# Two partial products in the array's two row halves, and a new instruction sequence, in a gated S4D and spectral filter kernel

## The chip, the cores and the metric

The kernel runs on one core of one Trainium2 chip. The metric is the device time of one execution in microseconds. Three runs of the kernel before took 536.1 to 537.85 us, with a median of 536.78 us.

A core has five engines that each work through a list of instructions in order: PE (the matmul array, with its weight loads listed as PEld), DVE (vector), ACT (scalar), POOL (GpSimd) and SP (which only issues transfers here). They wait for each other by semaphores. PE writes to PSUM, which is divided into banks of 512 f32 columns by 128 partitions; DVE and ACT read the results out of it.

## The reference

For x of 2048 positions and 640 channels, a gate g mixes two long filters: an S4D state space convolution along the positions, whose kernel K is generated from 128 complex modes per channel, and a two-dimensional spectral filter.

```python
def _A_ref(u, log_A_real, A_imag, C_real, C_imag, log_dt, D_skip):
    dt = jnp.exp(log_dt)
    A = -jnp.exp(log_A_real) + 1j * A_imag
    C = (C_real + 1j * C_imag) * dt[:, None]
    P = jnp.exp((A * dt[:, None])[:, :, None] * pos[None, None, :])
    K = 2.0 * jnp.einsum("dn,dnl->dl", C, P).real
    y = irfft(rfft(u_t, 2 * L) * rfft(K, 2 * L))[:, :, :L]
    return y + u * D_skip

def _B_ref(x, w_r, w_i):
    X = rfft2(x, axes=(-2, -1)) * (w_r + 1j * w_i)
    return irfft2(X, s=(S, D), axes=(-2, -1))

g = sigmoid((x * gate_w).sum(-1, keepdims=True))
return g * _A_ref(x, ...) + (1 - g) * _B_ref(x, ...)
```

## The kernel before

All Fourier transforms are products with constant tables in f32 on PE. The transform of 4096 points along the positions is factored into 32 x 64 plus a table: `stage1` (L367) and `stage2` (L380) make it, and the inverse is L886 followed by L960 and L172.

The program has these parts. `phase_p` turns the S4D parameters into phases and magnitudes, by DVE and POOL, with an exponential, an arctangent and a logarithm on ACT (L309, L326, L349). `phase_b` generates K in 40 steps: L696 and L706 make arguments on PE in bf16, L697, L712 and L718 take exponentials and sines on ACT, L726 to L732 multiply on DVE and POOL, L745 sums on PE. `phase_a` transforms u (four quarters of the channels, two u tiles each) and sums the gate (L454). Its copies out of PSUM are at L415, on ACT for the first two quarters. `phase_c` and `phase_d` transform K, multiply, go back, and mix.

The second half of `phase_a` is the spectral filter, and this is where the change lies. It runs over nine groups of up to 128 rows (17 blocks of 64). `front` loads a group and folds its 640 channels by symmetry into four planes of 321 numbers, 161 of one symmetry and 160 of the other. `transposes` (L550) brings these onto partitions, in three chunks that `CH` names: 0 to 128, 193 to 321, and the rest 128 to 193. The rest holds the last 33 rows of the first symmetry and the first 32 of the second, 65 rows together. `channels` makes the transform of the channels: for each of the four planes one bank `p_d`, with two results of 161 and 160 columns in it. Each result is a product over a full chunk (L566, 128 rows) plus a product over the 65-row rest (L567), whose table has zeros where the other symmetry lies. ACT copies two of the four banks (L571), DVE adds and subtracts the others (L573, L576). `filt` multiplies by the filter on DVE and folds again (L598, L599, and one column by POOL at L597). The way back is the same: `transposes` with `back=True`, `back1` with L611 (full) and L612 (rest) into `p_eo`, a copy on ACT (L615) and two DVE instructions (L617, L618) that make `qq`; then `back2` (L626, L627) and a transfer. The pool behind `p_t`, `p_d`, `p_eo` and `p_i` has three banks.

```python
v = p[:nl, 161 * par:161 + 160 * par]
P.matmul(v, st.ft[:, c, x, :nl], tab[0], start=True, stop=False)
P.matmul(v, st.ft[:65, 2, x, :nl], tab[1], start=False, stop=True)
```

The shape in which the array is used differs along PE's list: whole for L550, L566, L567, L611, L612 and L626, two row halves of 64 for L696 and L706 (two records, `j` 0 and 1, on partitions 0 and 64, into two banks), two column halves for L367, L380 and L886, four column quarters for L745 and L454.

The order of the instructions on each engine isn't that of the code. `arrange` takes tables, `ORDER` for each engine and `CROSS` between engines, and chains all instructions as they say. So every stream above is interleaved by hand-laid tables, and the tables are different for the two kernels.

Of the kernel before, what the change touches and what calls it, by code (L numbers as in the profile page):

```python
# [9 lines left out]
F32 = mybir.dt.float32  # L10
# [3 lines left out]
ALU = mybir.AluOpType  # L14
# [29 lines left out]
CH = ((0, 128), (193, 321), (128, 193))  # L44
# [5 lines left out]
def _tables():  # L50
# [45 lines left out]
    def chunks(t, part):  # L96
        z = np.zeros((161, t.shape[1]))
# [287 lines left out]
def phase_a(tc, A, T):  # L385
# [97 lines left out]
    with ExitStack() as ctx:  # L483
# [11 lines left out]
        for n in (161, 160) * 4:  # L495
            tabs.append((td[:, o:o + n], td[0:65, o + n:o + 2 * n]))
            o += 2 * n
# [5 lines left out]
        def bank(name):  # L503
            return ps.tile([128, 512], F32, tag="f", name=name)

        def tile5(name, n=E):
            return w4.tile([128, 4, E + 1], F32, tag="f", name=name)[:, :, 0:n]

        def front(pr, st):
# [12 lines left out]
            st.fo = wg.tile([128, 4, E], F32, tag="fg", name="fg")  # L522
            fg = st.fo.rearrange("p (t r) e -> p t r e", t=2)

            def folds(eng, t):
                ins = eng.tensor_tensor(out=fg[:nl, t, :, 1:160], in0=fo[:nl, t, :, 1:160], in1=fo[:nl, t, :, 319:160:-1], op=ALU.add)
                eng.tensor_tensor(out=fg[:nl, t, :, 162:321], in0=fo[:nl, 1 - t, :, 1:160], in1=fo[:nl, 1 - t, :, 319:160:-1], op=ALU.subtract)
# [29 lines left out]

        def channels(st, rest):
            nl = st.nl
            bc = wb.tile([128, 2, E], F32, tag="bc", name="bc")  # L560
            xx = st.xx = tile5("xx").rearrange("p (a b) e -> p a b e", a=2)
            for dst, x, w in ((0, 3, 1), (1, 2, 1), (2, 0, 0), (3, 1, 0)):
                p = bank("p_d")
                for par, (tab, c) in enumerate(fwd[w]):
                    v = p[:nl, 161 * par:161 + 160 * par]
                    P.matmul(v, st.ft[:, c, x, :nl], tab[0], start=True, stop=False)  # L566
                    P.matmul(v, st.ft[:65, 2, x, :nl], tab[1], start=False, stop=True)  # L567
                    yield 0.54
                i = dst % 2
                if dst < 2:  # L570
                    S.copy(bc[:nl, i], p[:nl, :E])  # L571
                else:
                    ins = V.tensor_tensor(out=xx[:nl, 0, i], in0=p[:nl, :E], in1=bc[:nl, i], op=ALU.add)  # L573
                    if dst == 2 and rest:
                        rest(ins)
                    V.tensor_tensor(out=xx[:nl, 1, i], in0=p[:nl, :E], in1=bc[:nl, i], op=ALU.subtract)  # L576

        def filt(st):
# [15 lines left out]
            ff = st.pm = tile5("ff")  # L594
            half = lambda t, i, n: t[:nl, :, i:i + 2 * n].rearrange("p x (b i) -> p x b i", b=2)
            lo, hi = half(pm, 0, 161)[:, :, :, 0:80], half(pm, 1, 160)[:, :, :, :79:-1]
            G.tensor_copy(ff[:nl, :, 160], pm[:nl, :, 80])  # L597
            V.tensor_tensor(out=half(ff, 0, 80), in0=lo, in1=hi, op=ALU.add)  # L598
            V.tensor_tensor(out=half(ff, 161, 80), in0=lo, in1=hi, op=ALU.subtract)  # L599

        def back1(st, j):
# [4 lines left out]
            blocks = lambda t, i, n: t[:, i:i + 2 * n].rearrange("p (b i) -> p b i", b=2)[:, :, 0:160]  # L606
            for w in (1, 0):
                p = bank("p_eo")
                for par, (tab, c) in enumerate(bwd[w]):
                    v = p[:, 161 * par:161 + 160 * par]  # L610
                    P.matmul(v, st.pmt[:, c, w, j, :], tab[0], start=True, stop=False)  # L611
                    P.matmul(v, st.pmt[:65, 2, w, j, :], tab[1], start=False, stop=True)  # L612
                    yield 0.57
                if w:
                    S.copy(o[:, :E], p[:, :E])  # L615
                else:
                    V.scalar_tensor_tensor(out=qv[:, :, 0:160], in0=blocks(o, 0, 161), scalar=T.sg[0], in1=blocks(p, 0, 161), op0=ALU.mult, op1=ALU.add)  # L617
                    V.scalar_tensor_tensor(out=qv[:, :, 319:159:-1], in0=blocks(o, 1, 160), scalar=T.sg[1], in1=blocks(p, 1, 160), op0=ALU.mult, op1=ALU.add)  # L618
# [521 lines left out]
```

## Time and profile before

| what | us |
|---|---|
| median of three runs | 536.78 |
| profiled execution | 540.0 |
| its span, first to last instruction | 538.2 |
| PE busy | 498.8 |
| DVE busy | 421.6 |
| ACT busy | 306.7 |
| POOL busy | 271.0 |

Busy times overlap between engines, so they don't add up to the span. A busy PE is not a PE at its peak: the records of matmuls are pipelined, and each one's duration is longer than the distance to the next. A row of the timeline has the start, the duration of a run of equal instructions, the engine, the line, the operation, what is written and read, the count, and in brackets how long the engine had stood idle before and who ended that. An f32 product is one instruction of the program and two records in the profile.

### The profile page before, as it was taken

The numbers are of one execution on the slowest core, as the hardware profiler recorded it, in microseconds if no ns is written. First come the engines' busy times: TensorE is split into PE (matmuls) and PEld (weight loads), VectorE is DVE, ScalarE is ACT, GpSimd is POOL, SyncE is SP. The second block draws the span as 40 slices with busy tenths as digits, with TensorE's granted clock in tenths as the row PEclk, the third lists the DMA queues.
The fourth block names the chain that finished last, engine by engine and source line by source line (L and its number), as shares of the span: only waits on it lengthen the run. The fifth ranks groups of instructions, "written<-read, shape, count | busy, mean of one in ns | idle before, by whom it ended". The sixth has DMA issues, their size and how long they took to land.

```text
span 538.2 us, 17116 instructions
## 1 busy us (share of the span) xinstructions
PE 498.8 (93%) x7432; PEld 382.1 (71%) x7432; DVE 421.6 (78%) x644; ACT 306.7 (57%) x469; POOL 271.0 (50%) x285
## 2 busy tenths in 40 slices
PE   6499999998889999999999999999999999998865
PEld 4489957765657767767667777667989988975621
DVE  0895448767989998989799789763797979887853
ACT  2386375564985887886977976876333333322100
POOL 4059827246355437375265363173553627674840
PEclk9699999999979999999999999999999999998997
DMA  8665933165550250553322231157779797698964
GB/s 339 233 212 184 333 138 130 46 206 173 187 199 13 63 166 6 167 182 97 83 62 71 99 111 27 55 212 307 263 252 329 258 357 234 191 384 334 311 226 182
DMA packets 47666, 99.89 MB, mean 186 GB/s; under 512 B 3588, under 2 KB 33048, under 8 KB 45928
## 3 DMA queue, kind: packets, MB, share of 16 engines
q1 hardware_dynamic: 25544, 67.08, 36.1%
q10 hardware_dynamic: 19552, 22.19, 12.7%
q0 software_dynamic: 2496, 9.54, 5.1%
q8 instruction: 58, 0.95, 0.8%
q14 instruction: 16, 0.13, 0.1%
HBM read 59.47 MB, written 38.99 MB: 183 GB/s over the span
## 4 chain that ended last, share of the span: by engine, by line
PE 74%; DMA 11%; ACT 7%; DVE 5%; issue 2%; ACTq 1%; POOL 0%; DVEq 0%; SPq 0%; POOLq 0%
PE p_s L367 13%; PE p_s L380 12%; PE p_p L706 8%; PE p_k L745 6%; PE p_i L886 6%; PE p_d L566 4%; PE p_i L626 4%; PE p_t L550 4%; PE p_d L567 3%; PE p_eo L611 3%; DMA s_d<-s 3%; PE p_e L696 3%; PE p_c L960 3%; PE p_eo L612 3%; DMA t<-s_d 2%; DMA lar<-in_la_l 2%
## 5 line engine op out<-in xcount | busy, mean ns | idle before, releaser
L380 PE MATMUL p_s<-t,w 128*64 128x160 f32 x1056 | 88.4, 306 | 0.8 <-ACT ut L415 0.7
L380 PEld LDWEIGHTS p_s<-t,w 128*64 128x64 f32 x1056 | 75.0, 135 | 11.8 <-issue 4.4
L731 POOL TENSOR_TENSOR y<-e,sc 128x512 f32<-128x512 f32 x40 | 52.1, 1303 | 30.1 <-ACT sc L712 24.5
L697 ACT ACTIVATE e<-p_e 128x1024 f32<-128x1024 f32 (+1 forms) x80 | 61.9, 818 | 7.8 <-PE p_e L696 4.9
L732 POOL TENSOR_TENSOR y<-e,sc 128x512 f32<-128x512 f32 x40 | 52.5, 1314 | 26.8 <-ACT sc L712 23.0
L706 PE MATMUL p_p<-rp,par 64*128 64x512 bf16 x480 | 62.6, 384 | 3.6 <-DVE x L728 3.5
L718 ACT ACTIVATE p_p<-p_p 128x1024 f32<-128x1024 f32 x40 | 40.4, 1010 | 34.2 <-PE p_p L706 23.7
L368 ACT COPY t<-p_s 128x512 f32<-128x512 f32 x40 | 25.1, 627 | 50.8 <-PE p_s L367 49.2
L367 PE MATMUL p_s<-c,u 128*64 128x128 f32 x640 | 41.3, 285 | 10.3 <-ACT t L415 9.5
L728 DVE TENSOR_TENSOR x<-e,p_p 128x1024 f32<-128x1024 f32 x40 | 48.5, 1212 | 0.0
L367 PEld LDWEIGHTS p_s<-c,u 128*64 128x64 f32 x640 | 37.7, 143 | 13.9 <-ACT t L415 9.7
L862 POOL TENSOR_TENSOR t<-ma 64x320 f32<-64x320 f32 x32 | 28.6, 893 | 36.0 <-DVE ma L856 34.6
L745 PEld LDWEIGHTS p_k<-x,y 128*32 128x32 f32 x2560 | 37.6, 110 | 10.8 <-issue 10.4
L726 DVE SCALAR_TENSOR_TENSOR x<-e,p_p 128x512 f32<-128x512 f32 x40 | 27.3, 682 | 22.8 <-ACT p_p L718 22.7
L367 PE MATMUL p_s<-c,kt 128*64 128x128 f32 x640 | 42.7, 274 | 2.2 <-DVE mb L857 1.0
L745 PE MATMUL p_k<-x,y 128*32 128x64 f32 x2560 | 44.0, 220 | 0.7 <-ACT kt L751 0.7
L888 ACT COPY s<-p_i 128x640 f32<-128x640 f32 x32 | 21.9, 693 | 38.3 <-PE p_i L886 28.3
L712 ACT ACTIVATE sc<-p_p 128x1024 f32<-128x1024 f32 x40 | 40.9, 1023 | 4.2 <-PE p_p L706 3.9
L886 PE MATMUL p_i<-t,w 128*64 128x160 f32 x528 | 41.9, 300 | 0.4 <-POOL t L862 0.3
L367 PEld LDWEIGHTS p_s<-c,kt 128*64 128x64 f32 x640 | 37.8, 136 | 5.6 <-issue 3.9
L706 PEld LDWEIGHTS <-par 64*128 64x128 bf16 x480 | 20.5, 95 | 29.6 <-issue 11.9
L886 PEld LDWEIGHTS p_i<-t,w 128*64 128x64 f32 x528 | 36.4, 136 | 4.1 <-POOL t L862 1.8
(163 smaller groups left out, 1063.4 us busy)
## 6 DMA issues: line engine op xcount, KB each, us to landing
u_d<-ut SPq DMA_DIRECT2D x32, 320.0 KB, 4.3
us<-u_d ACTq DMA_DIRECT2D x16, 640.0 KB, 7.8
s_d<-s ACTq DMA_DIRECT2D x15, 640.0 KB, 9.4
t<-s_d SPq DMA_DIRECT2D x14, 640.0 KB, 8.6
ww<-in_w_l SPq DMA_DIRECT2D x8, 642.0 KB
ue<-u_d SPq DMA_DIRECT2D x8, 640.0 KB
k_d<-kt SPq DMA_DIRECT2D x4, 1280.0 KB, 8.7
kt<-k_d SPq DMA_DIRECT2D x8, 640.0 KB, 5.8
```

Source lines behind the costliest of these rows:

```text
L367: nc.tensor.matmul(p[64 * ri:64 * ri + 64, j, :], src(i + j), e1[ri], start=True, stop=True)
L380: ins = nc.tensor.matmul(p[64 * j:64 * j + 64, i, 160 * ri:160 * ri + 160], w2[:, x, 64 * ri:64 * ri + 64], t1[:, x // 2 if x < 32 else K0 ...
L697: st.exp = S.activation(ef[:, :, c:c + n], p[:, :, 0:n], AF.Exp)
L706: P.matmul(p[:, j, 0:n], pars[0][t][x], w[x, y:y + n], start=i == 0, stop=i == 2)
L712: S.activation(sc.rearrange("p d v i -> p (d v i)"), p.rearrange("p j w -> p (j w)"), AF.Sin, scale=TWO_PI)
L718: T.trig = st.trig = S.activation(f, f, AF.Sin, scale=TWO_PI)
L728: V.tensor_tensor(out=x[:, 0].rearrange("p d (h j) -> p d h j", h=2), in0=e[:, :, 0:64].rearrange("p d (h j) -> p d h j", h=2), in1=cx.uns ...
L731: G.tensor_tensor(out=y[:, 1], in0=e[:, :, 64:96], in1=sc[:, 0], op=ALU.mult)
L732: G.tensor_tensor(out=y[:, 0], in0=e[:, :, 64:96], in1=sc[:, 1], op=ALU.mult)
L745: P.matmul(st.pb[32 * r:32 * r + 32, o, :], y[:, ri, 4 * qq + JR[r], :], x[:, ri, 4 * qq + JR[r], :], start=t % 2 + qq + 1 - ri == 0, stop ...
L862: return eng.tensor_tensor(out=t2[64 * im:64 * im + 64, o, :], in0=m[l, :hn, 0, :], in1=m[l, :hn, 1, :], op=ALU.add if im else ALU.subtract)
L886: T.mm = P.matmul(p[x:x + 64, i // 2, 160 * (i % 2):160 * (i % 2) + 160], T.w3[:, k0 + h + i, x:x + 64], t2[:, h + i, :], start=True, stop ...
```

## The change

The rest is laid out so that the 33 rows of the first symmetry lie on partitions 0 to 32 and the 32 rows of the second on 64 to 95. The planes become 352 wide (`FW`), the second symmetry begins at 192, and the third chunk is 97 columns, 128 to 225. What lies between (columns 161 to 191, and the row next to the 32) meets zeros in the tables. Two rest products, one per symmetry, then use different row halves of the array and different banks. For this, a bank holds one symmetry's result for two planes, not both results of one plane.

```diff
-CH = ((0, 128), (193, 321), (128, 193))
+CH = ((0, 128), (224, 352), (128, 225))
+FW = 352
...
     def chunks(t, part):
-        full = np.concatenate([t, z[:160]] if part == 0 else [z, t[:160]])
-        tail = np.concatenate([full[128:193], np.zeros((63, t.shape[1]))])
-        return [full[0:128] if part == 0 else full[193:321], tail]
+        tail = np.zeros((128, t.shape[1]))
+        if part:
+            tail[64:96] = t[0:32]
+            return [t[32:160], tail]
+        tail[0:33] = t[128:161]
+        return [t[0:128], tail]
...
-                G.tensor_copy(fg[:nl, :, :, 0:161:160], fo[:nl, :, :, 0:161:160])
-                G.tensor_copy(fg[:nl, :, :, 161], fo[:nl, ::-1, :, 0])
+                G.tensor_copy(fg[:nl, :, :, 0], fo[:nl, :, :, 0])
+                G.tensor_copy(fg[:nl, :, :, 160:192], fo[:nl, :, :, 160:192])
+                G.tensor_copy(fg[:nl, :, :, 192], fo[:nl, ::-1, :, 0])
...
+        def quads(items):
+            def product(it, rows, first):
+                out, src, (tab, c) = it
+                if rows:
+                    r = slice(64 * c, 64 * c + 33)
+                    P.matmul(out, src(2)[r], tab[1][r], start=first, stop=not first)
+                else:
+                    P.matmul(out, src(c), tab[0], start=first, stop=not first)
+            for i, rows, first in ((0, 0, True), (0, 1, False), (1, 1, True), (1, 0, False)):
+                for it in sorted(items[i], key=lambda it: it[2][1]):
+                    product(it, rows, first)
...
-            for dst, x, w in ((0, 3, 1), (1, 2, 1), (2, 0, 0), (3, 1, 0)):
-                p = bank("p_d")
-                for par, (tab, c) in enumerate(fwd[w]):
-                    v = p[:nl, 161 * par:161 + 160 * par]
-                    P.matmul(v, st.ft[:, c, x, :nl], tab[0], start=True, stop=False)
-                    P.matmul(v, st.ft[:65, 2, x, :nl], tab[1], start=False, stop=True)
+            for w, xs in ((1, (3, 2)), (0, (0, 1))):
+                pp = bank("p_d"), bank("p_d")
+                quads([[(pp[par][:nl, 161 * i:161 * i + 161 - par], (lambda c, x=x: st.ft[:, c, x, :nl]), fwd[w][par]) for par in range(2)] for i, x in enumerate(xs)])
+                for par, p in enumerate(pp):
+                    cut = slice(161 * par, 161 + 160 * par)
+                    v = p[:nl, 0:322].rearrange("p (i e) -> p i e", i=2)[:, :, 0:161 - par]
+                    if w:
+                        S.copy(bc[:nl, :, cut], v)
+                        continue
+                    ins = V.tensor_tensor(out=xx[:nl, 0, :, cut], in0=v, in1=bc[:nl, :, cut], op=ALU.add)
+                    V.tensor_tensor(out=xx[:nl, 1, :, cut], in0=v, in1=bc[:nl, :, cut], op=ALU.subtract)
...
-            G.tensor_copy(ff[:nl, :, 160], pm[:nl, :, 80])
+            G.tensor_copy(ff[:nl, :, 160:192], pm[:nl, :, 80:112])
...
-                if w:
-                    S.copy(o[:, :E], p[:, :E])
-                else:
-                    V.scalar_tensor_tensor(out=qv[:, :, 0:160], in0=blocks(o, 0, 161), scalar=T.sg[0], in1=blocks(p, 0, 161), op0=ALU.mult, op1=ALU.add)
-                    V.scalar_tensor_tensor(out=qv[:, :, 319:159:-1], in0=blocks(o, 1, 160), scalar=T.sg[1], in1=blocks(p, 1, 160), op0=ALU.mult, op1=ALU.add)
+            pp = bank("p_eo"), bank("p_eo")
+            quads([[(pp[c][:, 161 * i:161 * i + 161 - par], (lambda c, w=w: st.pmt[:, c, w, j, :]), (tab, c)) for par, (tab, c) in enumerate(bwd[w])] for i, w in enumerate((1, 0))])
+            for par in range(2):
+                S.copy(o[:, 161 * par:161 + 160 * par], pp[1 - par][:, 0:161 - par])
+            for par in range(2):
+                e = 161 * par
+                V.scalar_tensor_tensor(out=qv[:, par, 0:160], in0=o[:, e:e + 160], scalar=T.sg[0], in1=pp[par][:, 161:321], op0=ALU.mult, op1=ALU.add)
+                V.scalar_tensor_tensor(out=qv[:, par, 319:159:-1], in0=o[:, e + 1 - par:e + 161 - par], scalar=T.sg[1], in1=pp[par][:, 162 - par:322 - par], op0=ALU.mult, op1=ALU.add)
...
 ORDER = {
...
 CROSS = """
...
```

`ORDER` and `CROSS` are replaced as a whole. The line numbers of the changed kernel are 3 to 13 higher: L415 is L418 there, L309 is L312, and the products of `channels` and `back1` are L570 (full) and L568 (rest) for both.

Three places show how the instructions moved. The first is ACT near the program's start, where `t` and `ut` are the results of `stage1` and `stage2` for the first quarter of u, `lar` is a parameter (its row is the exponential) and `ph` the arctangent. Before:

```order
L415 COPY t_121<-p_s_216 128x16x16x2
L309 ACTIVATE lar<-lar 128x640
L415 COPY t_121<-p_s_226 128x16x16x2
L415 COPY t_121<-p_s_236 128x16x16x2
L459 COPY lg<-p_g 128x64
L415 COPY t_121<-p_s_272 128x16x16x2
L326 ACT_TABLE_LOAD
L326 ACTIVATE ph<-q 128x640
```

And in the changed kernel:

```order
L418 COPY ut<-p_s_381 128x320
L312 ACTIVATE lar<-lar 128x640
L418 COPY ut<-p_s_424 128x320
L418 COPY ut<-p_s_418 128x320
L418 COPY ut<-p_s_432 128x320
L418 COPY ut<-p_s_438 128x320
L329 ACT_TABLE_LOAD
L329 ACTIVATE ph<-q 128x640
```

The exponential stood behind the third copy of the first quarter's `stage1`; now it stands behind all ten of them, two copies of the gate's sums and six copies of `stage2`.

The second place is SP's first transfers, which feed these steps (`u` the input, `w_69` the table w2 of L380 in three pieces, `ld`, `ci`, `cr`, `ai`, `lar` the parameters). Before:

```order
L422 DMA u<-in_u_l 128x384
L422 DMA u<-in_u_l 128x896
L443 DMA w_69<-in_t_w 128x1408
L422 DMA u<-in_u_l 128x1280
L266 DMA ci<-in_ci_l 128x640
L266 DMA cr<-in_cr_l 128x640
L443 DMA w_69<-in_t_w 128x1408 x2
L266 DMA ai<-in_ai_l 128x640
L266 DMA lar<-in_la_l 128x640
```

And in the changed kernel:

```order
L425 DMA u<-in_u_l 128x384
L425 DMA u<-in_u_l 128x896
L425 DMA u<-in_u_l 128x1280
L446 DMA w_69<-in_t_w 128x1408 x2
L265 DMA ld<-in_ld_l 128x5
L269 DMA ci<-in_ci_l 128x640
L269 DMA cr<-in_cr_l 128x640
L446 DMA w_69<-in_t_w 128x1408
L269 DMA lar<-in_la_l 128x640
```

The second u tile moved ahead of the table, `ld` ahead of `ci`, and `lar` ahead of `ai`.

The third place is PE in the spectral stage, at a `back1` whose products stand together (`p_eo` with its buffer's number, `td` the tables, `pmt` the transposed planes). Before, two planes after each other, four products each:

```order
L611 MATMUL p_eo_3168<-td_1967,pmt_3078 128x161
L612 MATMUL p_eo_3168<-td_1967,pmt_3078 128x161
L611 MATMUL p_eo_3168<-td_1967,pmt_3078 128x160
L612 MATMUL p_eo_3168<-td_1967,pmt_3078 128x160
```

And in the changed kernel, both planes in one group:

```order
L570 MATMUL p_eo_2304<-td_1967,pmt_2251 128x160
L570 MATMUL p_eo_2305<-td_1967,pmt_2251 128x161
L568 MATMUL p_eo_2304<-td_1967,pmt_2251 128x160
L568 MATMUL p_eo_2305<-td_1967,pmt_2251 128x161
L568 MATMUL p_eo_2304<-td_1967,pmt_2251 128x161
L568 MATMUL p_eo_2305<-td_1967,pmt_2251 128x160
L570 MATMUL p_eo_2304<-td_1967,pmt_2251 128x161
L570 MATMUL p_eo_2305<-td_1967,pmt_2251 128x160
```

A full and a rest product took turns in one bank; now two full ones, four rests that alternate between two banks and row halves, and two full ones follow each other.

More of the change, by code (lines that the diff above doesn't have):

```diff
@@ L506, in tile5 @@
         def tile5(name, n=E):
-            return w4.tile([128, 4, E + 1], F32, tag="f", name=name)[:, :, 0:n]
+            return w4.tile([128, 4, FW], F32, tag="f", name=name)[:, :, 0:n]
         def front(pr, st):
@@ L521, in front @@
             V.tensor_tensor(out=fo[:nl, 1].rearrange("p r (c d) -> p r c d", c=2), in0=ue[:nl, :, 0:2], in1=ue[:nl, :, 2:4], op=ALU.subtract)
-            st.fo = wg.tile([128, 4, E], F32, tag="fg", name="fg")
+            st.fo = wg.tile([128, 4, FW], F32, tag="fg", name="fg")
             fg = st.fo.rearrange("p (t r) e -> p t r e", t=2)
@@ L526, in folds @@
                 ins = eng.tensor_tensor(out=fg[:nl, t, :, 1:160], in0=fo[:nl, t, :, 1:160], in1=fo[:nl, t, :, 319:160:-1], op=ALU.add)
[L527 removed]
+                eng.tensor_tensor(out=fg[:nl, t, :, 193:352], in0=fo[:nl, 1 - t, :, 1:160], in1=fo[:nl, 1 - t, :, 319:160:-1], op=ALU.subtract)
                 return ins
@@ L561, in channels @@
             xx = st.xx = tile5("xx").rearrange("p (a b) e -> p a b e", a=2)
-            for dst, x, w in ((0, 3, 1), (1, 2, 1), (2, 0, 0), (3, 1, 0)):
-                p = bank("p_d")
-                for par, (tab, c) in enumerate(fwd[w]):
-                    v = p[:nl, 161 * par:161 + 160 * par]
-                    P.matmul(v, st.ft[:, c, x, :nl], tab[0], start=True, stop=False)
[L567 to L571, printed above, removed]
-                else:
-                    ins = V.tensor_tensor(out=xx[:nl, 0, i], in0=p[:nl, :E], in1=bc[:nl, i], op=ALU.add)
-                    if dst == 2 and rest:
+            for w, xs in ((1, (3, 2)), (0, (0, 1))):
+                pp = bank("p_d"), bank("p_d")
+                quads([[(pp[par][:nl, 161 * i:161 * i + 161 - par], (lambda c, x=x: st.ft[:, c, x, :nl]), fwd[w][par]) for par in range(2)] for i, x in enumerate(xs)])
+                yield 1.7
+                for par, p in enumerate(pp):
[5 more added lines that the diff above has]
+                    ins = V.tensor_tensor(out=xx[:nl, 0, :, cut], in0=v, in1=bc[:nl, :, cut], op=ALU.add)
+                    if par == 0 and rest:
                         rest(ins)
-                    V.tensor_tensor(out=xx[:nl, 1, i], in0=p[:nl, :E], in1=bc[:nl, i], op=ALU.subtract)
+                    V.tensor_tensor(out=xx[:nl, 1, :, cut], in0=v, in1=bc[:nl, :, cut], op=ALU.subtract)
         def filt(st):
@@ L605, in back1 @@
             qv = qq.rearrange("p (i b) -> p b i", b=2)
[L606 to L613, printed above, removed]
-                if w:
-                    S.copy(o[:, :E], p[:, :E])
-                else:
-                    V.scalar_tensor_tensor(out=qv[:, :, 0:160], in0=blocks(o, 0, 161), scalar=T.sg[0], in1=blocks(p, 0, 161), op0=ALU.mult, op1=ALU.add)
-                    V.scalar_tensor_tensor(out=qv[:, :, 319:159:-1], in0=blocks(o, 1, 160), scalar=T.sg[1], in1=blocks(p, 1, 160), op0=ALU.mult, op1=ALU.add)
+            pp = bank("p_eo"), bank("p_eo")
+            quads([[(pp[c][:, 161 * i:161 * i + 161 - par], (lambda c, w=w: st.pmt[:, c, w, j, :]), (tab, c)) for par, (tab, c) in enumerate(bwd[w])] for i, w in enumerate((1, 0))])
+            yield 1.7
+            for par in range(2):
[4 more added lines that the diff above has]
+                V.scalar_tensor_tensor(out=qv[:, par, 319:159:-1], in0=o[:, e + 1 - par:e + 161 - par], scalar=T.sg[1], in1=pp[par][:, 162 - par:322 - par], op0=ALU.mult, op1=ALU.add)
         def back2(st, pr, j):
```

31 lines of the change are left out of this document (14 added, 17 removed), and 102 rows, old and new, of the table ORDER.

## The prediction

> **What bounds the kernel now.** I read the busy time by stretches first, then the waits, then the chain of work that ended last. The stretches (columns: busy time of PE, PEld, DVE, ACT, POOL with instruction counts, granted clock, DMA share, GB/s):
>
> ```profile
> 0.00:30.00 30.00, 17.71 (x256) 14.38 (x258) 15.93 (x30) 10.80 (x17) 6.44 (x11) 0.83 0.68 257
> 30.00:138.00 108.00, 103.31 (x1952) 81.45 (x1951) 74.07 (x115) 66.74 (x102) 64.81 (x61) 1.00 0.53 181
> 138.00:366.00 228.00, 221.89 (x3222) 159.84 (x3210) 202.00 (x299) 179.79 (x274) 111.59 (x117) 0.99 0.34 109
> 366.00:480.00 114.00, 112.48 (x1680) 101.73 (x1682) 91.00 (x135) 43.22 (x69) 62.04 (x71) 1.00 0.83 280
> 480.00:538.00 58.00, 43.38 (x346) 24.67 (x342) 38.62 (x69) 6.12 (x10) 26.08 (x28) 0.91 0.77 272
> ```
>
> From 30 to 480 us the matmul engine is busy for all but 12 of 450 us. The spectral stage, where the edited products lie, is the third stretch: 228 us, with the vector engine a close second at 202. The chain says the same for the whole span:
>
> ```profile
> PE 74%; DMA 11%; ACT 7%; DVE 5%; issue 2%; ACTq 1%; POOL 0%; DVEq 0%; SPq 0%; POOLq 0%
> ```
>
> The first 30 us are the loose part. The longest single waits of PE and of ACT are one event, and the timeline shows it:
>
> ```profile
> PE p_s L367 <- ACT t L415: 9.5, 1, 9.5
> ACT lar L309 <- DMA lar<-in_la_l: 10.7, 1, 10.7
> ...
> 5.97 4.59 PE L367 MATMUL p_s<-c,u 128*64 128x128 f32 x80 [0.74 <-DMA c<-in_t_c]
> 11.08 0.77 PE L454 MATMUL p_g<-u,z 128*32 128x64 f32 x40 [0.52 <-POOL z L427]
> 12.97 0.85 DVE L317 TENSOR_SCALAR ab<-ci 128x640 int32<-128x640 int32 x1 [11.41 <-DMA ci<-in_ci_l]
> 20.11 0.74 ACT L309 ACTIVATE lar<-lar 128x640 f32<-128x640 f32 x1 [10.66 <-DMA lar<-in_la_l]
> 21.38 7.00 PE L367 MATMUL p_s<-c,u 128*64 128x128 f32 x80 [9.53 <-ACT t L415]
> 25.32 0.74 ACT L326 ACTIVATE ph<-q 128x640 f32<-128x640 f32 x1
> 29.12 1.07 PE L380 MATMUL p_s<-t,w 128*64 128x160 f32 x12
> ```
>
> ACT works in order. The exponential at L309, behind three copies, waits for the last parameter load until 20.11; the PSUM copies behind it wait too, the three banks fill, and PE stands still from 11.85 (11.08 + 0.77) to 21.38.
>
> **The new sequence at the start.** In the changed order the exponential stands fifteen copies later on ACT and the second u tile ahead of all of the w2 table on SP. When is PE ready for that tile? At 11.85. Even in the old order the tile was queued ahead of ci, and ci had landed at 12.97, so it costs at most 1.1 us. The second group of L367 then takes 4.6 us, as the first did, instead of 7.0 (an arctangent and its table sat among its copies), the 40 gate records 0.8, and L380 can start near 17.2 instead of 29.12: 11.9 us at best. Part comes back. The arctangent now stands among the copies of L380's first 17 products, and its input q comes from DVE, which now runs the small ld instructions first. Nothing ahead of q was taken away there, so I let the arctangent end near 26 as before (25.32 + 0.74); seven of these copies still lie behind it, three of them in banks already filled, so PE may lose 2 us there and as much again at the logarithm that follows, 2 to 5 us in all. I take 9.5 us, the wait that is listed, between 7 and 12. A second chain must keep up, the one of the parameters:
>
> ```profile
> 29.30 1.89 DVE L330 TENSOR_TENSOR ph<-ph,y 128x640 f32<-128x640 f32 x1
> 31.23 0.49 DVE L331 TENSOR_SCALAR y<-ph 128x640 f32<-128x640 f32 x1
> 33.67 1.43 POOL L310 TENSOR_TENSOR lar<-lar,dtn 128x640 f32<-128x640 f32 x1 [3.15 <-DVE dt L281]
> 68.74 0.39 PE L696 MATMUL p_e<-rm,par 48*128 48x512 bf16 x2
> ```
>
> L310 waited for DVE's dtn. That now stands right behind the reciprocal and ex, with twelve full-width instructions such as L330 and L331 (0.49 to 1.89 us each) moved behind it, some 9 us; so what feeds L696 moves about as far as PE does.
>
> **The products.** One f32 product is two records, and in steady state products start 0.275 us apart (219.32, 219.59, 219.86):
>
> ```profile
> 216.66 0.82 PE L706 MATMUL p_p<-rp,par 64*128 64x512 bf16 x6
> 217.32 0.38 PE L696 MATMUL p_e<-rm,par 48*128 48x512 bf16 x2
> 217.63 1.10 PE L745 MATMUL p_k<-x,y 128*32 128x64 f32 x64
> ...
> 219.32 0.43 PE L611 MATMUL p_eo<-td,pmt 128*128 128x160 f32 x2
> 219.59 0.44 PE L612 MATMUL p_eo<-td,pmt 65*128 65x160 f32 x2
> 219.86 0.44 PE L611 MATMUL p_eo<-td,pmt 128*128 128x161 f32 x2
> ...
> L567 PE MATMUL p_d<-td,ft x144: 297/299/475, 140.4 to 336.8; 65*128 65x161 f32 x64, 65*128 65x160 f32 x64, 65*64 65x161 f32 x8, 65*64 65x160 f32 x8
> L612 PE MATMUL p_eo<-td,pmt x136: 297/299/404, 167.5 to 358.8; 65*128 65x161 f32 x68, 65*128 65x160 f32 x68
> ```
>
> The 65-row rests are 280 records, 140 products, 38.5 us. Do two row halves run at once? L706 already works so: six records take from 216.66 to 217.32, 0.22 for each two, and the next two (L696) begin right on time. That is bf16; f32 in row halves has no row here, but f32 in four column tiles does: 64 records of L745 pass in 1.03 us (217.63 to 218.66), 0.016 each, while a lone record of 160 columns takes half of 0.275, by its columns 0.055 for 64: some four run at once. So I expect pairs: 70 x 0.275 = 19.2 us less. The price is the change of the array's shape. L696 to L745 is 0.31 instead of 0.22, so 0.09, and the chain gives the same from two batches of L706:
>
> ```profile
> 211.01 1.40 PE p_p L706 x12
> 216.73 0.75 PE p_p L706 x6
> ```
>
> Six more records cost 0.65, so 0.10 of each batch is the change of shape. Each of the 35 groups of eight products now goes full, halves, full. Counted along PE's order, changes of shape grow from 257 to 300: 43 x 0.10 = 4.3 us. PE's load falls by 19.2 - 4.3 = 14.9 us. [...]
>
> **The evacuations.** The two halves of a product now lie in two banks, so what read one bank reads two:
>
> ```profile
> L617 DVE SCALAR_TENSOR_TENSOR qq<-o,c,p_eo 128x320 f32<-128x320 f32 x17 | 9.2, 543 | 2.2 <-PE p_eo L612 2.2
> L963 DVE SCALAR_TENSOR_TENSOR ot<-p_c,gate,oe 128x160 f32<-128x160 f32 x16 | 5.1, 377 | 8.0 <-PE p_c L960 7.8
> L615 ACT COPY o<-p_eo 128x321 f32<-128x321 f32 x17 | 7.2, 432 | 7.6 <-PE p_eo L612 7.5
> L890 ACT COPY s<-p_i 128x160 f32<-128x160 f32 x4 | 1.2, 294 | 7.2 <-PE p_i L886 7.2
> L573 DVE TENSOR_TENSOR xx<-p_d,bc 128x321 f32<-128x321 f32 x16 | 7.8, 487 | 2.0 <-PE p_d L567 1.7
> L597 POOL COPY ff<-pm 128x4 f32<-128x4 f32 x8 | 4.1, 509 | 17.3 <-DVE pm L592 17.3
> ```
>
> DVE: 17 times four instructions of 160 columns instead of two of 320: 17 x (4 x 0.377 - 2 x 0.543) = 7.2 us more. ACT: 17 x (2 x 0.294 - 0.432) = 2.7 us more, under its 48 idle us of the stage. The four xx instructions keep their width (322 and 320 columns for 321). POOL: one copy more in nine fronts and wider ones; at 0.5 us about 5 to 9 us in a stage where POOL idles 116; if that cover fails, the third chunk of transposes is late by about 0.5 us in nine rounds.
>
> **The stage and the sum.** In the stage PE sheds 14.9 us and DVE gains 7.2, to 209.2. DVE alone would allow 228 - 209 = 19 us, PE's load 15; neither runs without gaps, and DVE's own idle time there is mostly behind PE:
>
> ```profile
> DVE x L726 <- ACT p_p L718: 12.5, 9, 4.7
> ACT p_p L718 <- PE p_p L706: 15.2, 16, 2.5
> ```
>
> So a faster PE shortens DVE's idle time as well. Bounds 0 and 15; I take 7, the middle, since two engines now run near their limits. The last two stretches do the same work; I give them nothing. Sum: 9.5 + 7 = 16.5 us. The profiled execution took 540.0 us (span 538.2), so 523.5 there; the median of the three runs lies 3.2 lower, 536.78 - 16.5 = 520.3 us.
>
> **The rivals.**
> (a) DVE takes over the stage: it keeps about 19 of its 26 idle us, so 209 + 19 = 228 and the stage gains nothing. For it: 92% load; against it: the waits above end on PE. 536.8 - 9.5 = 527.3 us. [...]
> (b) The early gain is taken back before 70 us because the parameters arrive late for L696; only the stage gains: 536.8 - 7 = 529.8 us.
> (c) The f32 halves run one after the other: no 19.2, but 4.3 more on PE: 536.8 - 9.5 + 4.3 = 531.6 us.
> (d) Slower: the pool behind p_t, p_d, p_eo and p_i keeps three banks, and a group now takes two at once and gives them back only after up to four evacuations (4 x 0.487 = 1.95 us). If each of the 35 groups holds PE for half of that, 0.97, the stage grows by 34 - 14.9 = 19 us, and the run takes 536.8 - 9.5 + 19 = 546 us. It decides from (14.9 + 9.5) / 35 = 0.70 us a group. Against it: other work stands between many groups in the order; for it: PE's order is fixed, and a late evacuation stops everything behind.
>
> **How the numbers follow.** Forecast 0.52, (a) 0.20, (b) 0.08, (c) 0.08, (d) 0.12. The forecast's own range is 536.8 - 27 to 536.8 - 7, 510 to 530. (a), (b) and (c) lie below 534, so 510 to 534 leaves out (d) and little else. About 0.3%, 1.6 us, can be told from no change here: faster means below 535.2. That holds all of the forecast and of (a), and most of (b) and (c): 0.85; same 0.03; slower 0.12.
>
> **What would show it.** Early: no wait of PE near 10 us, and L380 beginning at 17 to 22 us. Products: L568 in 64*128 with two records starting together, and PE's busy time in the stage lower by about 15. Evacuations: L630 and L631 near 377 ns, DVE's sum 7 us higher. If waits of the p_d and p_eo products for ACT or DVE copies are long, (d) is right; if the first L696 waits for its parameters by several us, (b); if the stage stays near 228 us with DVE above 95%, (a).

## The result, and the profile after

The changed kernel is slower. Its first four executions took 542.06 to 547.53 us (median 543.97) against 537.32 for the kernel before on the same chip: a ratio of 1.0112, 95% interval 1.0073 to 1.0151. In a second set, labelled `again` below, the ratio was 1.0092 [1.0056, 1.0127], so about 1.0% or 5.4 us. The profiled execution took 542.06 us (span 540.3); it was the fastest of its four, while the profiled one of before, at 540.0, lay above its median, so the two spans differ by only 2.1 us. Ratios leave out executions more than 1.5% above the fastest of their kernel: three of the twelve of `ff_on_pool` (with them its mean would be 540.2 us against 538.8 before, 0.3% above instead of 0.1% below) and one each of `less_dve`, `narrow_rests`, `narrow_less_dve` and, in the set of `ff_on_pool`, the kernel before. The stretches of the changed kernel, with the columns of the table in the prediction:

```profile
0.00:30.00 30.00, 25.73 (x387) 21.82 (x389) 16.30 (x31) 17.05 (x33) 11.89 (x14) 1.00 0.91 353
30.00:138.00 108.00, 99.40 (x1842) 77.80 (x1838) 87.99 (x120) 65.59 (x96) 61.38 (x61) 0.98 0.49 167
138.00:366.00 228.00, 214.49 (x3185) 139.71 (x3185) 206.22 (x325) 177.39 (x281) 117.66 (x122) 0.97 0.31 102
...
```

The early hole is filled (PE 25.7 of 30 us instead of 17.7). From 138 to 366 us PE is busy 7.4 us less and DVE 4.2 us more, but the two kernels don't do quite the same work between these two times. Where the time went is read best from a few starts in the timelines, in us (names of the changed kernel):

| | before | changed | again | tail_fix | exp_late |
|---|---|---|---|---|---|
| first L383 (`stage2`) | 29.1 | 18.2 | 18.7 | 18.5 | 17.4 |
| first L709 (arguments of `phase_b`) | 68.7 | 66.9 | 67.9 | 66.8 | 66.4 |
| first L741 (last x product of a step, DVE) | 83.8 | 83.8 | 84.8 | 83.7 | 81.5 |
| first L383 behind the spectral stage | 378.9 | 379.7 | 383.9 | 378.0 | 376.4 |
| last record of L899 (`p_i`) | 512.3 | 511.9 | 516.2 | 510.4 | 507.4 |
| end | 538.2 | 540.3 | 545.3 | 535.2 | 532.8 |

Four differences make up the 2.1 us of the two profiled executions. To the first x: 83.8 and 83.8, nothing left of the early gain. (PE has more behind it by then: 396 records of `stage2` instead of 350 and 515 of `stage1` instead of 480, but 12 of L719 instead of 18; by the spacing of these records some 5 us of work, an estimate. The x products come no earlier for it.) From there to the first L383 behind the stage: 295.1 and 295.9, +0.8. Then to the last `p_i`: 133.4 and 132.2, -1.2, where this profile of the kernel before has a half-clock spell of 3.4 us (from 494.0 us on) that the other has not. From there to the end: 25.9 and 28.4, +2.5.

Between the same two marks, the first x and the first L383 behind the stage, before and then changed:

```profile
83.81:378.88 295.07, 285.57 (x4597) 206.95 (x4593) 247.86 (x373) 218.26 (x322) 142.05 (x148) 0.99 0.36 120
83.81:379.70 295.89, 278.46 (x4522) 186.01 (x4517) 255.47 (x399) 223.50 (x340) 149.15 (x157) 0.98 0.35 117
```

PE is busy 7.1 us less and DVE 7.6 us more, and the stage is no shorter.

**The early lead is given back before 70 us.** PE, POOL and DVE of the changed kernel, from the timeline:

```profile
18.24 7.77 PE L383 MATMUL p_s<-t,w 128*64 128x160 f32 x104
...
34.09 1.97 PE L370 MATMUL p_s<-c,u 128*64 128x128 f32 x32 [1.79 <-ACT t L418]
...
58.26 3.51 PE L370 MATMUL p_s<-c,u 128*64 128x128 f32 x32 [3.77 <-DVE t L418]
66.92 0.50 PE L709 MATMUL p_e<-rm,par 48*128 48x512 bf16 x4
...
25.13 1.70 POOL L313 TENSOR_TENSOR lar<-lar,dtn 128x640 f32<-128x640 f32 x1 [4.72 <-DVE dtn L285]
...
46.59 1.42 POOL L293 TENSOR_TENSOR th<-th,parts 128x640 f32<-128x640 f32 x1
47.96 1.28 POOL L430 TENSOR_TENSOR z<-c,gw 128x640 f32<-128x640 f32 x1
...
54.99 1.39 POOL L293 TENSOR_TENSOR parts<-th,parts 128x640 bf16<-128x640 f32 x1
...
46.32 3.61 DVE L293 TENSOR_TENSOR q<-q,parts 128x640 f32<-128x640 f32 x1
52.12 0.82 DVE L293 TENSOR_TENSOR ph<-ph,parts 128x640 f32<-128x640 f32 x1
52.97 3.77 DVE L291 CAST parts<-ph 128x640 bf16<-128x640 f32 x1
56.77 0.82 DVE L293 TENSOR_TENSOR parts<-ph,parts 128x640 bf16<-128x640 f32 x1
57.52 1.88 DVE L418 COPY t<-p_s 128x512 f32<-128x512 f32 x3
```

PE is 10.9 us ahead at L383, and L313 starts 8.5 us earlier (25.13 against the 33.67 of L310 before): `dtn` came forward. The rest of the parameters did not. DVE's last row of them before, on the same scale:

```profile
53.93 1.92 DVE L290 TENSOR_TENSOR parts<-ph,parts 128x640 bf16<-128x640 f32 x1
```

So DVE was done with them at 55.9 us before and is at 57.6 now. From the third quarter on the copies out of PSUM are DVE's too, behind this work: PE waits 3.77 us for them. The 32 records behind that wait take 3.51 us, at a granted clock of 0.50 up to 61.3 us, where 32 such records took 1.97 at 34.09, at a clock of 1.00. PE had also waited 1.19 and 1.79 us for ACT's copies since L383 began (before, since L380: 0.72), and the new order puts 16 more records of L370 ahead of L709. What is left of the 10.9 us at L709 is 1.8. L709 itself has no wait for its parameters.

Why did DVE not come forward? Its reciprocal, at the head of the chain, started 3.4 us later (20.36 against 16.92), with the small `ld` instructions now among those ahead of it. Then DVE worked without the 6.1 us of waiting that it had before, but its instructions grew: the same form, L293, took 0.82 us in a gap of POOL and 3.61 while POOL ran L293 and L430 beside it, and the cast of L291 took 0.48 and 3.77. Both long rows end within 0.7 us of the last POOL row beside them (49.24 and 56.38). That POOL is the cause is read from such rows; no run here took POOL's work away.

**The row halves run at once, but the changes eat most of it.** One group of eight products, the records by line:

```profile
207.96 0.81 PE L570 MATMUL p_eo<-td,pmt 128*128 128x160 f32 x4
208.70 0.82 PE L568 MATMUL p_eo<-td,pmt 33*128 33x160 f32 x8
209.45 0.81 PE L570 MATMUL p_eo<-td,pmt 128*128 128x161 f32 x4
210.19 1.10 PE L758 MATMUL p_k<-x,y 128*32 128x64 f32 x64
```

Eight records of L568 pass in the time of four of L570, so they run in pairs. But each of the three parts takes 0.74 to 0.75 us, of which two products are 0.55: the group needs 2.23 us.

**What PE waits for in the spectral stage.** Of before, then of the changed kernel (us in total, times, longest):

```profile
PE p_e L696 <- ACT e L697: 1.5, 3, 0.6
PE p_d L566 <- ACT ft L555: 1.5, 2, 1.1
PE p_p L706 <- DVE x L728: 1.0, 2, 0.6
```

```profile
PE p_e L709 <- ACT e L710: 3.4, 5, 1.2
PE p_p L719 <- DVE x L741: 2.4, 2, 1.7
PE p_e L709 <- DVE x L741: 1.6, 4, 0.7
PE p_p L719 <- ACT e L710: 1.4, 2, 0.9
PE p_p L719 <- ACT sc L725: 1.2, 1, 1.2
PE p_t L554 <- DVE qq L631: 1.0, 1, 1.0
PE p_i L639 <- DVE xx L593: 0.8, 1, 0.8
PE p_eo L570 <- DVE qq L631: 0.8, 1, 0.8
```

The waits for DVE and ACT went from about 5 us to 13. 10.0 of the 13 belong to `phase_b`, whose next arguments need banks that must first have been read: 4.0 by the x products on DVE, 6.0 by ACT's exponentials and sines (`e`, `sc`). The waits behind the two-bank groups (the last three rows) sum to 2.6 us.

**The tail.** ACT and PE of the changed kernel at the end:

```profile
514.80 0.53 ACTq L948 DMA_DIRECT2D t<-s_d  x1
515.37 0.69 ACT L901 COPY s<-p_i 128x640 f32<-128x640 f32 x1 [2.47 <-DMA t<-s]
...
510.79 1.39 PE L899 MATMUL p_i<-t,w 128*64 128x160 f32 x16 [0.40 <-POOL t L875]
528.45 4.36 PE L973 MATMUL p_c<-t,c 128*64 128x480 f32 x12 [12.16 <-DMA out<-ot]
```

The last `p_i` is ready at 512.2 (510.79 + 1.39), its copy starts at 515.37: in the new order the load L948 stands on ACT ahead of this copy, where the kernel before has it behind.

### The profile page after: what moved, and what is told of

The parts are those of the page before. It is cut to its first block, busy times and chain, and to the rows that moved or that the text cites. A ratio compares the mean times of both kernels' runs of the same rounds, so it can differ in the third digit from the quotient of the medians.

```text
span 540.3 us, 17163 instructions
## 1 busy us (share of the span) xinstructions
PE 492.6 (91%) x7432; PEld 368.6 (68%) x7432; DVE 439.1 (81%) x678; ACT 310.3 (57%) x486; POOL 279.0 (52%) x294
## 4 chain that ended last, share of the span: by engine, by line
PE 37%; DVE 10%; DMA 4%; issue 1%; ACT 1%; POOL 1%; ACTq 0%; SPq 0%; DVEq 0%; POOLq 0%
PE p_s L383 7%; PE p_s L370 7%; PE p_i L899 6%; PE p_e L175 3%; PE p_c L973 3%; PE p_p L719 3%; PE p_k L758 2%; PE p_i L639 2%; DMA out<-ot 1%; PE p_t L554 1%; DMA kt<-k_d 1%; DVE x L741 1%; PE p_d L570 1%; PE p_eo L570 1%; DMA t<-s 1%
## 5 line engine op out<-in xcount | busy, mean ns | idle before, releaser
L383 PE MATMUL p_s<-t,w 128*64 128x160 f32 x1056 | 89.6, 306 | 2.8 <-ACT ut L418 1.2
L383 PEld LDWEIGHTS p_s<-t,w 128*64 128x64 f32 x1056 | 76.2, 134 | 12.0 <-issue 2.9
L719 PE MATMUL p_p<-rp,par 64*128 64x512 bf16 x480 | 65.4, 396 | 7.6 <-DVE x L741 4.4
L744 POOL TENSOR_TENSOR y<-e,sc 128x512 f32<-128x512 f32 x40 | 53.8, 1347 | 31.6 <-ACT sc L725 31.6
L745 POOL TENSOR_TENSOR y<-e,sc 128x512 f32<-128x512 f32 x40 | 56.0, 1403 | 19.0 <-ACT sc L725 19.0
L731 ACT ACTIVATE p_p<-p_p 128x1024 f32<-128x1024 f32 x40 | 40.5, 1012 | 23.0 <-PE p_p L719 18.5
L741 DVE TENSOR_TENSOR x<-e,p_p 128x1024 f32<-128x1024 f32 x40 | 48.5, 1213 | 0.0
L370 PE MATMUL p_s<-c,u 128*64 128x128 f32 x640 | 40.4, 284 | 5.8 <-DVE t L418 3.8
L758 PEld LDWEIGHTS p_k<-x,y 128*32 128x32 f32 x2560 | 37.6, 110 | 11.6 <-issue 9.5
L719 PEld LDWEIGHTS <-par 64*128 64x128 bf16 x480 | 21.4, 97 | 34.1 <-issue 14.7
L370 PE MATMUL p_s<-c,kt 128*64 128x128 f32 x640 | 43.8, 274 | 0.4 <-POOL kt L820 0.2
L899 PE MATMUL p_i<-t,w 128*64 128x160 f32 x528 | 42.7, 300 | 1.4 <-DVE mb L870 0.5
L758 PE MATMUL p_k<-x,y 128*32 128x64 f32 x2560 | 43.8, 220 | 0.1
L370 PEld LDWEIGHTS p_s<-c,u 128*64 128x64 f32 x640 | 37.5, 143 | 9.1 <-DVE t L418 4.4
L370 PEld LDWEIGHTS p_s<-c,kt 128*64 128x64 f32 x640 | 39.3, 136 | 3.4 <-issue 1.4
L899 PEld LDWEIGHTS p_i<-t,w 128*64 128x64 f32 x528 | 37.2, 136 | 4.4 <-issue 2.3
L739 DVE SCALAR_TENSOR_TENSOR x<-e,p_p 128x512 f32<-128x512 f32 x40 | 27.3, 682 | 15.1 <-ACT p_p L731 14.9
```

The source lines that it names most:

```text
L370: nc.tensor.matmul(p[64 * ri:64 * ri + 64, j, :], src(i + j), e1[ri], start=True, stop=True)
L383: ins = nc.tensor.matmul(p[64 * j:64 * j + 64, i, 160 * ri:160 * ri + 160], w2[:, x, 64 * ri:64 * ri + 64], t1[:, x // 2 if x < 32 else K0 ...
L719: P.matmul(p[:, j, 0:n], pars[0][t][x], w[x, y:y + n], start=i == 0, stop=i == 2)
L731: T.trig = st.trig = S.activation(f, f, AF.Sin, scale=TWO_PI)
L741: V.tensor_tensor(out=x[:, 0].rearrange("p d (h j) -> p d h j", h=2), in0=e[:, :, 0:64].rearrange("p d (h j) -> p d h j", h=2), in1=cx.uns ...
L744: G.tensor_tensor(out=y[:, 1], in0=e[:, :, 64:96], in1=sc[:, 0], op=ALU.mult)
```

## The experiments

Each is named as in the table. Ratios are to the kernel before, run on the same chip in the same set.

**whole_rests**: the row halves taken out of the changed kernel.

```diff
-                    r = slice(64 * c, 64 * c + 33)
+                    r = slice(0, 97)
```

> The changed kernel, with each rest product over all 97 rows of the third chunk instead of 33 in one row half (the other symmetry's rows of the table are zero, so the same sums); same order, counts and layout, no row halves and no change of shape inside a group of eight. By the changed kernel's trace a group is three stretches of 0.74 to 0.75 us (0.55 of stream and 0.19 to 0.20 of change each), 2.23; with whole rests it is one change and 8 x 0.275, 2.40: 35 groups x 0.17 = 6 us more on PE. Theory (from 138 to 366 us PE no longer sets the pace alone, its freed time is idle): 0 to +2 us against the changed kernel. Rival 1 (PE sets it): +6. Rival 2 (as predicted, a change costs 0.10, so the halves are worth 35 x (0.55 - 0.20)): +12.

Measured: 1.0134 [1.0092, 1.0177], against 1.0112 and 1.0092 for the changed kernel. PE's timeline, the same group:

```profile
208.54 1.47 PE L719 MATMUL p_p<-rp,par 64*128 64x512 bf16 x12
209.94 0.81 PE L570 MATMUL p_eo<-td,pmt 128*128 128x160 f32 x4
210.58 1.26 PE L568 MATMUL p_eo<-td,pmt 97*128 97x160 f32 x8
211.68 0.71 PE L570 MATMUL p_eo<-td,pmt 128*128 128x161 f32 x4
212.32 1.10 PE L758 MATMUL p_k<-x,y 128*32 128x64 f32 x64
```

The group takes 2.38 us, so the halves save 0.15 in a group like this. 20 of the 35 groups stand undivided; the others are divided by other work. Summed over all 35, without PE's idle time, the stretches of these products take 85.7 us here and 79.1 with the halves (by the trace of `tail_fix`), so the halves save some 6.5 us.

Without changes inside, 0.09 us (0.64 - 0.55) is lost behind the group's first record and as much ahead of L758; the two changes inside the other group then cost 0.20 each (2.23 - 1.65 - 0.18, by two). The change into the group, from the bf16 halves of L719, costs no less. Its first part lies ahead of the group: twelve records of L719 take 1.40 us up to 209.94, twice the 0.65 of six would be 1.30. With the 0.09 behind the first record that is 0.19.

The time rose by 1 to 2 us, and from the first x to the first L383 the profiled execution took 300.1 us. Rival 2 is out. Between the theory and rival 1 the intervals hardly decide: PE's work still counts, but not in full.

**tail_fix**: ACT's last entries in the order of before.

```diff
-498+8 509 506 508 507
+498+9 508 507 509
```

> The changed kernel, with the load of the last t3 rows (L948) issued on ACT behind the last p_i copy and its two stores instead of ahead of them, as the kernel before has it. Theory (the load's wait holds ACT, so the last copy starts 2.5 us late and the final p_c with it): 2 to 3.5 us less than the changed kernel (542 to 541). Rival (the end waits for the load's own landing, whatever stands behind it on ACT): within 1 us.

Measured: 1.0031 [1.0002, 1.0060], about 0.7% or 3.8 us below the changed kernel. Its ACT and PE:

```profile
510.72 0.69 ACT L901 COPY s<-p_i 128x640 f32<-128x640 f32 x1 [1.85 <-PE p_i L899]
513.24 0.53 ACTq L948 DMA_DIRECT2D t<-s_d  x1
...
523.47 3.90 PE L973 MATMUL p_c<-t,c 128*64 128x480 f32 x12 [8.68 <-DMA t<-s_d]
```

The last copy now starts when its product ends, and the way from the last `p_i` to the end is 24.8 us instead of 28.4 (29.1 in `again`). The theory holds. Its size is less sure: the same stretch takes 26.8 to 29.2 us in the six profiles with the load ahead, 24.8 and 26.7 in the two with it behind (`tail_fix`, `ff_on_pool`), and the two ratios compared have intervals of 0.3 to 0.4% each.

**exp_late**: the kernel before, with ACT's exponential behind the early copies.

```diff
-1 0 2 4+3 3 7+4 22 11+5 33 16+6 23+10 34+34
+1 0 2 4+18 3 23+4 22 27+6 34 33 35+33
```

> The kernel before, with nothing but ACT's early order altered: Exp (L309) stands behind all copies of the first two transforms, as the changed kernel has it, and the two activations behind it (L326, L349) follow. Theory (PE's early lead is real but is worth nothing, because the stage that ends the first part, phase_b on DVE and ACT, does not start or run earlier): L380 starts 7 to 12 us earlier (about 18 to 22 instead of 29.1), the first x on DVE within 1.5 us of 83.8, the time within 1.5 us of the kernel before. Rival (as predicted): the time falls by 9.5 us, 7 to 12.

Measured: 0.9980 [0.9954, 1.0006]. PE's timeline:

```profile
17.37 7.59 PE L380 MATMUL p_s<-t,w 128*64 128x160 f32 x104
...
66.41 0.39 PE L696 MATMUL p_e<-rm,par 48*128 48x512 bf16 x2 [1.41 <-DMA par<-par_d]
```

L380 starts 11.7 us earlier, the first L696 2.3 us earlier, and there PE waits for its parameters' transfer. The first x follows 2.3 us earlier, a little more than the theory allowed, and the lead stays about there to the end of the stage (376.4 against 378.9). An early lead of PE of 11.7 us is worth 1 us, at most 2.5.

**less_dve** and **before_less_dve**: less DVE work in the changed kernel, and in the kernel before.

```diff
-            V.tensor_tensor(out=mm[:nl, 0], in0=xx[:nl, 0], in1=ww[:nl, 3:1:-1], op=ALU.mult)
-            V.tensor_tensor(out=mm[:nl, 1], in0=xx[:nl, 1], in1=ww[:nl, 1::-1], op=ALU.mult)
+            V.tensor_tensor(out=mm[:nl, 0, :, 0:8], in0=xx[:nl, 0, :, 0:8], in1=ww[:nl, 3:1:-1, 0:8], op=ALU.mult)
+            V.tensor_tensor(out=mm[:nl, 1, :, 0:8], in0=xx[:nl, 1, :, 0:8], in1=ww[:nl, 1::-1, 0:8], op=ALU.mult)
```

> The changed kernel, with the second pair of products in filt (18 DVE instructions of 2x321 elements) cut to 8 of 321 columns: the rest of that pair is left out, so its sums use the first pair's values. DVE loses about 18 x 0.7 = 12.6 us of SBUF-only work between 138 and 366; PE, ACT and POOL lose nothing. Theory (DVE shares the bound of that stretch): 5 to 12 us less than the changed kernel. Rival 1 (PE still sets it): within 1.5 us. Rival 2 (a chain that runs PE, ACT, DVE in turn through phase_b sets it, and filt lies beside it): 0 to 3 us less.

> The kernel before, with the second pair of products in filt cut to 8 of 321 columns (the rest of that pair is left out). DVE loses about 10 us between 138 and 366, as the same cut took from the changed kernel (206.2 to 197.9). Theory (before the change PE set that stretch, after it PE and DVE share it): within 2 us of the kernel before, where the cut gave the changed kernel some 5 us. Rival (DVE was as much of a bound before): 4 us less or more.

Measured: 0.9970 [0.9940, 1.0001] for the changed kernel so cut, 1.3% or 7 us below it; 0.9981 [0.9955, 1.0007] for the kernel before, 1 us. The busy times of whole executions of the changed kernel, `less_dve` and `before_less_dve` (the kernel before has DVE at 421.6):

```profile
PE 492.6 (91%) x7432; PEld 368.6 (68%) x7432; DVE 439.1 (81%) x678; ACT 310.3 (57%) x486; POOL 279.0 (52%) x294
PE 490.3 (91%) x7432; PEld 366.3 (68%) x7432; DVE 428.9 (80%) x678; ACT 310.2 (58%) x486; POOL 274.9 (51%) x294
PE 498.5 (93%) x7432; PEld 383.3 (72%) x7432; DVE 412.0 (77%) x644; ACT 306.6 (57%) x469; POOL 272.3 (51%) x285
```

DVE lost 10.2 us in the changed kernel and 9.6 in the kernel before. (Between 138 and 366 us `less_dve` shows only 8.3 less, because it gets further in that time.) The same cut is worth about 0.7 us per us of DVE after the change (0.5 to 0.9) and 0.1 before it (up to 0.25): DVE has become a bound.

**narrow_rests** and **narrow_less_dve**: less PE work in the changed kernel, alone and with the cut of `less_dve`.

```diff
-                    P.matmul(out, src(2)[r], tab[1][r], start=first, stop=not first)
+                    m = slice(0, None if first else 16)
+                    P.matmul(out[:, m], src(2)[r], tab[1][r, m], start=first, stop=not first)
```

> The changed kernel, with the two rest products that come second in each group of eight cut to 16 of 160 or 161 columns (the sums of the other columns miss these rests). PE loses about 35 x 0.25 = 8.7 us of stream between 122 and 366, no instruction and no change of shape. Theory (freed PE time there turns into waiting for DVE x and ACT e): 0 to 3 us less than the changed kernel, PE's idle share up by 6 to 9 us. Rival (PE sets the pace): 7 to 9 us less.

> The changed kernel with both cuts, the narrow rests on PE and the cut products on DVE. Theory (the two engines share the bound): clearly more than the sum of the two cuts alone, 8 to 14 us less than the changed kernel. Rival 1 (DVE alone sets it): as the DVE cut alone, 3 to 7 us less. Rival 2 (a chain through ACT sets it): no more than 5 us less.

Measured: 1.0019 [0.9986, 1.0053], some 4.4 us below the changed kernel, and 0.9918 [0.9879, 0.9957], 9.9 us below it. But the edit did less than was expected of it. PE's timeline of `narrow_rests`, one group:

```profile
205.99 0.81 PE L571 MATMUL p_eo<-td,pmt 128*128 128x160 f32 x4
206.74 0.77 PE L569 MATMUL p_eo<-td,pmt 33*128 33x16 f32 x8
...
208.17 1.10 PE L759 MATMUL p_k<-x,y 128*32 128x64 f32 x64
```

With the narrow records the group takes 2.18 us instead of 2.23, not 1.98. Summed over the 35 groups as for `whole_rests`, PE lost 3.2 us (79.1 to 75.9, by the trace of `narrow_less_dve`), not 8.7, so neither theory nor rival was put to its test. It can still be set against `whole_rests`: between the two lie 9.7 us of PE's work and 1.15% or 6.2 us of time, so a us of PE is worth about two thirds, with intervals that allow from a third to nearly all. The second run is in the theory's range, but not more than the sum of the two cuts (4.4 + 7): the two add up. So, as far as these intervals go, neither engine sets the stage alone: PE's work counts at about two thirds, DVE's at about 0.7.

**again**: the changed kernel unaltered.

> The changed kernel unaltered, as the base for the others of this set. Its loss has so far been seen in few executions: 1.0112 [1.0073, 1.0151]. Theory (2.5 us of it is ACT's tail, the rest comes from executions in which PE's clock is granted at half for some 3 to 4 us after new idle stretches, near 240 and 274 us): 1.006 to 1.012, with a spread of single executions of over 4 us. Rival (the first result was a draw from a wide spread): below 1.005.

Measured: 1.0092 [1.0056, 1.0127], 541.95 to 547.1 us. The spread has a place. `again` and then `tail_fix`, which are one program up to the tail (PE's timeline, and one row of the stretches):

```profile
237.71 1.29 PE L719 MATMUL p_p<-rp,par 64*128 64x512 bf16 x6 [1.22 <-ACT sc L725]
240.22 2.74 PE L719 MATMUL p_p<-rp,par 64*128 64x512 bf16 x12 [1.22 <-DVE x L741]
...
238.00:240.00 2.00, 1.00 (x6) 0.10 (x2) 2.00 (x3) 1.01 (x2) 2.00 (x3) 0.50 0.26 108
```

```profile
236.48 0.82 PE L719 MATMUL p_p<-rp,par 64*128 64x512 bf16 x6 [1.22 <-ACT sc L725]
238.99 1.47 PE L719 MATMUL p_p<-rp,par 64*128 64x512 bf16 x12 [1.69 <-DVE x L741]
```

In both, PE stands idle twice here, waiting for ACT and DVE. In `again` the granted clock is 0.50 from 238 us on: the same six records take 1.29 us instead of 0.82, the same twelve 2.74 instead of 1.47. Such half-clock spells, 3.4 or 6.8 us long, near 240 and between 271 and 286 us are in the profiles of the changed kernel (2), `again` (2), `less_dve` (2), `narrow_rests` (1) and `ff_on_pool` (2), not in `tail_fix`, `whole_rests` and `narrow_less_dve`, and in none of the three with the order of before (before, `exp_late`, `before_less_dve`). All profiles have one near 155, and most have others ahead of 130 or behind 490 us. What tells the two sets apart is PE's idle stretches: between 138 and 366 us all eight profiles with the new order have 14 or 15 of 0.4 us or more, the three with the old one 6 or 7. The row halves are not needed for them: `whole_rests` has 14.

From the first x to the first L383 the profiled `again` took 299.1 us, `tail_fix` 294.3. So the spells cost time, but they aren't why the stage gained nothing: without them `tail_fix` needs 294.3 us against 295.1 before. Near 240 us the same instructions ran at a granted clock of 0.50 in one execution (238 to 244 us) and at 1.00 in the other (236 to 246 us); no run here shows why.

**ff_on_pool**: an attempt to take load off DVE with nothing left out, on top of `tail_fix`. `AFTER` has the places in POOL's list behind which the moved instructions go.

```diff
-            V.tensor_tensor(out=half(ff, 192, 80), in0=lo, in1=hi, op=ALU.subtract)
+            T.moved.append(G.tensor_tensor(out=half(ff, 192, 80), in0=lo, in1=hi, op=ALU.subtract))
...
+AFTER = [77, 96, 107, 121, 130, 141, 160, 176, 179]
...
```

> The changed kernel with the tail mended (the load behind the last copy, as in tail_fix) and, in each of the nine rounds, the second of filt's two folds into ff (L616, 128x640) issued on POOL instead of DVE: behind POOL's copy of the same round, in two rounds behind the next y products. Nothing is left out. DVE loses 9 x 0.82 = 7.4 us between 138 and 366, POOL (118 us busy there) gains 9 x 1.3 to 1.9. Theory (with the change DVE co-sets that stretch; cutting 9.7 us of its work gave some 7 us): 3 to 6 us less than tail_fix, so 0.992 to 0.998 of the kernel before, and the stretch from the first x on DVE to the first s2 of the third stretch 2 to 5 us shorter than tail_fix's 294.3. Rival 1 (what POOL takes over slows DVE beside it as much as it frees): within 1.5 us of tail_fix, DVE's other SBUF instructions longer by some 5 us in sum. Rival 2 (the y products on POOL come late): slower than tail_fix.

Measured: 0.9993 [0.9959, 1.0027], 2 us below `tail_fix` with intervals that overlap: inconclusive between theory and rival 1. DVE gave up 6.6 us, not 7.4 (439.1 to 432.5 in the whole execution), since the fold that stays on DVE slowed from 0.895 to 1.088 us beside its twin:

```profile
L616 DVE TENSOR_TENSOR ff<-pm 128x640 f32<-128x640 f32 (+1 forms) x9 | 9.8, 1088 | 0.0
```

No version here that leaves nothing out beats the kernel before by more than its interval; `exp_late` comes nearest.

## Why the prediction was wrong

Forecast: 520.3 us, 510 to 534, faster at 0.85. The time lies outside the range, and the sign is wrong.

- **The early term (9.5 us) was right about PE and wrong about its worth.** PE started L383 10.9 us earlier. The step that failed is "so what feeds L696 moves about as far as PE does". I argued from the place of `dtn` in DVE's list, and `dtn` did come 8.5 us earlier. What counted was when DVE finishes all of the parameters, since PE's copies stand behind them: 57.6 us instead of 55.9, with instructions that stretched beside POOL's. Rival (b) had the outcome right, but not the path: L709 didn't wait for its parameters, PE was held by DVE's copies before it. `exp_late` shows it without the rest of the change: 11.7 us of lead on PE, 2.3 at the first x, 1 us in the time.
- **"0.10 of each batch is the change of shape" was half of what it costs here.** I took it from bf16 batches, where only the part ahead of the next line's start shows. Pairs of rests do run at once, as forecast (rival (c) is out), but a change into a stretch of these f32 products costs 0.19 to 0.20, about half of it behind the first record. The 70 changes inside the groups take back 14 of the 19.2 us. With the 27 fewer changes elsewhere (70 more and 43 net), at 0.09 to 0.20 each, PE's load falls by 7.6 to 10.6 us (an estimate) instead of 14.9; between the two marks of the stage PE is busy 7.1 us less.
- **"I take 7, the middle" was the wrong end.** From the first x on, the stage gained nothing. The DVE term was exact (L630 and L631 at 376 and 375 ns, 377 forecast; DVE as a whole is busy 7.6 us more between the two marks), and rival (a) was right that the stage gains nothing, but not in its bookkeeping: DVE didn't end at 228 us busy. DVE and PE share the bound, so that part of PE's freed time became waits for x, e and sc. Before the change, a cut on DVE was worth 0.1 us per us; after it, 0.7. By the prices of the experiments (an estimate), 9 us less on PE at two thirds are worth 6 us, and 7.6 us more on DVE at 0.7 cost 5: little is left.
- **"The last two stretches do the same work; I give them nothing" missed ACT's tail.** I didn't follow what else moved in the new order there. One load ahead of one copy cost some 2.5 us by the profiles and 3.8 by the times, whose intervals cover both; `tail_fix` shows it.
- **Rival (d)**, evacuations that hold PE, is there at 2.6 us, not 34. The slower sign came from other places.
- **Not thought of at all**: idle stretches of PE and half-clock spells behind some of them. The new order has more of both, by the profiles, with row halves or without. How much of the mean time the spells cost isn't measured apart; in `again` against `tail_fix` they and the waits around them made 4.8 us of the stage.

After the tail is mended, 0.31% [0.02, 0.60] remains of the loss: a stage that gained nothing, and an early lead that was worth nothing.

## What to carry to other kernels

Before taking load off the busiest engine, ask what the change adds to the second busiest. A cut tried on the kernel before doesn't answer that: 10 us off DVE were worth 0.1 us per us there and 0.7 after the change. Ask with the first engine's load already lightened, or add the new work to the kernel before (no run here did that). A lead at the start is worth only what the last input of the next stage gains. When an order is laid out anew, follow each engine's last few entries as well as the place that was meant: a load that waits, one place ahead of a copy, cost as much here as anything else.

## What was not expected of the hardware

- A change of the array's shape ahead of f32 products of 160 columns cost 0.19 to 0.20 us, between whole array and row halves and from bf16 halves into the whole array; only about half of it shows ahead of the first record. Narrowing a pair of such products to 16 columns saved 0.05 us in a group, not 0.25.
- Two DVE instructions took more than four times as long while POOL ran L293 and L430 beside them as their like did in a gap of POOL: L293 3.61 against 0.82 us, and a cast, L291, 3.77 against 0.48. That POOL is the cause was not shown apart.
- PE's granted clock was 0.50 right after one idle stretch of 1.22 us (`again`, from 238 us on), and in another execution of the same code (`tail_fix`), with idle stretches of 1.22 and 1.69 us at the same place, it was 1.00.
